# Two attention layers and two gated layers on one core: token statistics moved ahead of phi, transposes one unit ahead, and the copies of k^T v times output weights on ScalarE alone

## The chip, the cores and the metric

The kernel runs on one core of one Trainium2 chip. The time is device microseconds (us) of one execution, as a median of several. TensorE is the matmul engine, VectorE and ScalarE work element by element, GpSimd (POOL in the profile) does small vectors here, and a sequencer (SP) issues the DMA transfers. Each engine is given its own list of instructions, so a schedule is the order in which the program emits them.

## The reference, cut to what matters

```python
phi = lambda t: jnp.where(t > 0, t + 1, jnp.exp(t)) + 1e-6
pq, pk = phi(q), phi(k)
kv  = jnp.einsum("bhsd,bhse->bhde", pk, v)
num = jnp.einsum("bhqd,bhde->bhqe", pq, kv)
den = jnp.einsum("bhqd,bhd->bhq", pq, pk.sum(over tokens))    # shortened
attention(x) = (num / den) @ wo                               # 32 heads of 32
...
x = x + attention(layernorm(x));  x = x + gated(layernorm(x))   # and both once more
```

There are 2048 tokens of width 1024, in bf16. The kernel handles the tokens in 16 tiles of 128, in four groups of four tiles. A tile's layernorm needs its mean and variance ("token statistics") before the tile can be normalised, transposed and multiplied by the weights.

## The kernel before: the parts that the change touches

The k projection of a tile is two units, each eight matmuls, followed by phi on ScalarE (the exp) and VectorE (two instructions):

```python
def phi(ps, dst):
    e = work.tile([P, NB], BF16, tag="e", bufs=3, name="e")
    nc.scalar.activation(out=e[:], in_=ps[:], func=ACT.Exp)
    nc.vector.tensor_scalar(out=e[:], in0=e[:], scalar1=1.0, scalar2=1e-6, op0=ALU.min, op1=ALU.add)
    nc.vector.scalar_tensor_tensor(out=dst, in0=ps[:], scalar=1.0 + 1e-6, in1=e[:], op0=ALU.add, op1=ALU.max)
```

Statistics are made on VectorE (`bn` twice, then an aggregate) and finished on GpSimd (`rstd`). One tile of each later group has its statistics on ScalarE instead (`ln_stats_act`), with GpSimd between its two passes. Group 0 is normalised on VectorE and transposed on TensorE (`tx_pe`, with a ScalarE copy out of PSUM). The later groups are normalised on ScalarE, which first needs an offset from GpSimd, and transposed by a DMA (`tx`).

```python
def ln_apply_act(t, xn):
    mv, rstd = stat.pop(t)
    off = small.tile([P, 1], F32, tag="off", name="off")
    nc.gpsimd.tensor_scalar(out=off[:], in0=mv[:, 0:1], scalar1=rstd[:], scalar2=-1.0, op0=ALU.mult, op1=ALU.mult)
    nc.scalar.activation(out=xn, in_=X[:, t, :], func=ACT.Identity, scale=rstd[:], bias=off[:])
```

The first layer's order, from group 1 on (`u` are projections of the group before):

```python
for g in range(1, NG):
    t = g * TPG
    u = early if g == 1 else k[8 * g - 8:8 * g]
    ... # loads of later tiles of x
    ln_stats(t)
    ln_stats_act(t + 1, xn_a[t + 1])
    u[0]();  norm(t);      ln_stats(t + 2)
    u[1]();  norm(t + 1);  ln_stats(t + 3)
    u[2]();  norm(t + 2)
    ...
    u[3]();  norm(t + 3)
    do(u[4:])
do(k[8 * NG - 8:])
```

The second part that changes sits later in each attention layer. Sixteen single matmuls, k^T v times the output weights, are woven between the last q projections. Each result is copied out of PSUM, one in four by VectorE:

```python
def kvo_unit(c, n):
    ps = mm_tile()
    nc.tensor.matmul(out=ps[:], lhsT=KVT[0][:, c, :], rhs=wo[n][:, c, :], start=True, stop=True)
    if c % 4 == 3:
        nc.vector.tensor_copy(out=KVo[n][:, c, :], in_=ps[:])
    else:
        nc.scalar.copy(out=KVo[n][:, c, :], in_=ps[:])
```

All matmul results share eight PSUM buffers (`mm_tile`). VectorE is far behind at this point: each pair of q projections brings it some 4.3 us of division work besides the two phis of 0.9 us each, and takes TensorE 3.5 us.

## Time and profile before

| before | value |
|---|---|
| time | 1647.24 us, median of 3 (1647.19 to 1649.03) |
| span of the profiled run | 1646.2 us |
| busy: TensorE, VectorE, ScalarE, GpSimd | 1622.5, 646.2, 266.8, 58.0 us |
| mean granted TensorE clock | 0.999 |

TensorE is busy for 99% of the span, so the change can only touch the remaining 24 us, and the stretches in which TensorE's clock is low, which count as busy. The view that finds the waits is the list of waits of TensorE. Its columns are the waiting engine and line, what it waited for, the sum, the number of waits and the longest. This is the kernel before:

```profile
PE ps L233 <- DMA xT_71<-W_77: 3.9, 1, 3.9
PE ps L233 <- ACT xT_70 L215: 2.2, 2, 1.1
PE ps L233 <- DMA xT_73<-D_84: 2.2, 1, 2.2
...
PE ps L233 <- DVE pq L225: 1.1, 2, 0.5
PE ps L319 <- DVE D_80 L321: 1.1, 2, 0.5
PE pt L214 <- DVE W_76 L194: 0.6, 1, 0.6
PE ps L233 <- ACT D_81 L323: 0.6, 2, 0.3
```

L233 is a projection, xT_71 and xT_73 are the transposed tokens of groups 1 and 3, and L319 is one of the sixteen single matmuls. The four lines with xT or pt belong to the first layer. The other three occur once in each attention layer.

A list of waits does not say which wait sets the time. The chain of waits, followed back from the end, does. In the following piece of it for the kernel before, the columns are start, duration and engine with line, in time order:

```profile
29.01 1.21 DVE st L161 x2
30.24 0.22 DVE mv L165
...
30.83 0.66 POOL rstd L169
...
31.59 0.28 POOL off L201
...
33.04 0.59 ACT e L223
```

Up to 62.4 us the chain hardly touches TensorE after 14.5 us. It runs through statistics (st), GpSimd, ScalarE, phi on VectorE, and statistics again. TensorE's waits are where this chain hands work over.

The timeline of TensorE before shows when that happens. The columns are start, duration, engine, line, instruction, output and inputs, count, and in brackets the idle time before it with its releaser:

```profile
30.68 3.55 PE L233 MATMUL ps<-W_74,xT_71 128*128 128x512 bf16 x8 [3.94 <-DMA xT_71<-W_77]
...
62.37 1.90 PE L233 MATMUL ps<-W_74,xT_73 128*128 128x512 bf16 x8 [2.23 <-DMA xT_73<-D_84]
...
76.19 0.81 PE L245 MATMUL ps<-H,W_76 128*128 128x512 bf16 x3
...
184.22 1.03 PE L319 MATMUL ps<-H,kvt 128*128 128x512 bf16 x4
188.39 1.89 PE L233 MATMUL ps<-D_79,xT_73 128*128 128x512 bf16 x7 [0.55 <-DVE pq L225]
...
191.43 1.89 PE L233 MATMUL ps<-D_78,xT_73 128*128 128x512 bf16 x8 [0.30 <-ACT D_81 L323]
...
194.29 0.59 PE L319 MATMUL ps<-H,kvt 128*128 128x512 bf16 x2 [0.54 <-DVE D_80 L321]
...
196.69 5.34 PE L337 MATMUL ps<-D_80,xT_70 128*128 128x512 bf16 x23
```

Eight projection matmuls normally start 1.73 us before the next eight; after the 3.94 us wait it was 3.39 us, at a granted clock of 0.50 (30.7 to 34.0 us). The line at 76.19 us, the first matmul of x^T k, marks the end of the stage. From 184.22 us (the first single matmul) to 196.69 us (the output projection) TensorE needs 12.47 us.

### The profile page before, as it was taken

Reading aid. Unit: us, or ns where it says so; the run is one execution under the profiler, and the core shown is the slowest. Engines: PE = TensorE matmul, PEld = TensorE weight load, DVE = VectorE, ACT = ScalarE, POOL = GpSimd, SP = SyncE. Lnnn points to the kernel's source line nnn. Section 1 sums busy time; section 2 is a strip of 40 time slices with the busy share of each in tenths; the row PEclk is TensorE's granted clock in tenths of the full one; section 3 lists DMA queues with packets and bytes.
Section 4 is the critical chain, followed back from the end, with each engine's and each line's share of the span. In section 5 each row is a group of like instructions: output and inputs, shape, how many; then the busy total and the mean of one; then the engine's idle time right before and its main releaser. Section 6 shows DMA issues by size and latency. Waiting matters only on the chain.

```text
span 1646.2 us, 18145 instructions
## 1 busy us (share of the span) xinstructions
PE 1622.5 (99%) x7547; PEld 744.7 (45%) x7696; DVE 646.2 (39%) x1050; ACT 266.8 (16%) x444; POOL 58.0 (4%) x159
## 2 busy tenths in 40 slices
PE   8999999999999999999999999999999999999999
PEld 3444444444444444444444444444444444444444
DVE  5789964211311321122676889532132113111111
ACT  5522301100110110011023222011011101100110
POOL 2100000000000000000200000000000000000000
PEclk9999999999999999999999999999999999999999
DMA  5602729630641453041450135394226406421400
GB/s 166 167 13 45 192 40 315 189 102 6 177 152 49 112 170 103 0 154 51 108 149 1 32 71 153 98 336 154 67 68 172 157 23 167 152 78 64 154 4 23
DMA packets 245011, 182.59 MB, mean 111 GB/s; under 512 B 100545, under 2 KB 235713, under 8 KB 244929
## 3 DMA queue, kind: packets, MB, share of 16 engines
q1 hardware_dynamic: 244928, 181.43, 38.3%
q8 instruction: 60, 0.98, 0.3%
q14 instruction: 23, 0.18, 0.0%
HBM read 153.09 MB, written 4.19 MB: 96 GB/s over the span
## 4 chain that ended last, share of the span: by engine, by line
PE 94%; DVE 3%; issue 1%; ACT 1%; POOL 0%; DMA 0%; ACTq 0%; DVEq 0%
PE ps L351 47%; PE ps L368 23%; PE ps L233 10%; PE ps L337 7%; PE ps L245 7%; DVE st L161 1%; DVE H L225 1%; ACT e L223 0%; PE zps L153 0%; DVE pq L225 0%; DVE e L224 0%; DVE D_82 L289 0%; DVE den L291 0%; POOL rstd L169 0%; ACT D_81 L323 0%
## 5 line engine op out<-in xcount | busy, mean ns | idle before, releaser
L355 DVE TENSOR_TENSOR H<-gs,ps 128x512 bf16<-128x512 f32 x224 | 154.1, 688 | 575.2 <-PE ps L351 543.7
L354 ACT COPY gs<-ps 128x512 f32<-128x512 f32 x224 | 131.3, 586 | 1039.4 <-PE ps L351 1016.5
L368 PEld LDWEIGHTS <-H 128*128 128x128 bf16 x1848 | 178.6, 98 | 208.7
L370 DVE TENSOR_TENSOR X<-X,ps 128x512 bf16<-128x512 bf16 (+1 forms) x66 | 44.3, 672 | 319.7 <-PE ps L368 287.5
L223 ACT ACTIVATE e<-ps 128x512 bf16<-128x512 f32 x128 | 75.8, 595 | 174.7 <-PE ps L233 163.4
L351 PEld LDWEIGHTS <-W_75 128*128 128x128 bf16 x640 | 62.6, 98 | 75.5
L351 PEld LDWEIGHTS <-W_74 128*128 128x128 bf16 x640 | 62.6, 98 | 75.5
L351 PEld LDWEIGHTS <-xT_72 128*128 128x128 bf16 x576 | 56.4, 98 | 68.0
L351 PEld LDWEIGHTS <-W_76 128*128 128x128 bf16 x576 | 56.4, 98 | 68.0
L351 PEld LDWEIGHTS <-W_77 128*128 128x128 bf16 x576 | 56.4, 98 | 67.9
L351 PEld LDWEIGHTS <-xT_73 128*128 128x128 bf16 x576 | 56.4, 98 | 67.9
L161 DVE BATCH_NORM_STATS2 st<-X 128x6 f32<-128x512 bf16 x122 | 77.4, 675 | 2.3 <-DMA X<-in_A_x_dram 2.3
L351 PE MATMUL ps<-xT_70,xT_72 128*128 128x512 bf16 x314 | 75.3, 379 | 0.3
L351 PE MATMUL ps<-xT_71,W_76 128*128 128x512 bf16 x314 | 75.3, 379 | 0.3
L351 PE MATMUL ps<-xT_71,W_77 128*128 128x512 bf16 x312 | 75.2, 379 | 0.4
L351 PE MATMUL ps<-xT_70,xT_73 128*128 128x512 bf16 x316 | 75.4, 379 | 0.2
L351 PE MATMUL ps<-xT_70,W_74 128*128 128x512 bf16 x316 | 74.7, 379 | 0.3
L351 PE MATMUL ps<-xT_71,W_74 128*128 128x512 bf16 x314 | 74.6, 379 | 0.4
L351 PE MATMUL ps<-xT_71,W_75 128*128 128x512 bf16 x314 | 74.6, 379 | 0.3
L351 PE MATMUL ps<-xT_70,W_75 128*128 128x512 bf16 x312 | 74.2, 379 | 0.3
L368 PE MATMUL ps<-D_81,H 128*128 128x512 bf16 (+2 forms) x264 | 66.0, 373 | 0.4
L368 PE MATMUL ps<-D_78,H 128*128 128x512 bf16 (+2 forms) x262 | 65.9, 372 | 0.3
(127 smaller groups left out, 1817.1 us busy)
## 6 DMA issues: line engine op xcount, KB each, us to landing
W_74<-in_B_w_gate_dram SPq DMA_DIRECT2D x20, 1024.0 KB, 5.3
W_75<-in_B_w_up_dram SPq DMA_DIRECT2D x20, 1024.0 KB, 7.5
W_76<-in_B_w_gate_dram SPq DMA_DIRECT2D x18, 1024.0 KB, 5.3
W_77<-in_B_w_up_dram SPq DMA_DIRECT2D x18, 1024.0 KB, 7.5
xT_72<-in_B_w_gate_dram SPq DMA_DIRECT2D x18, 1024.0 KB, 5.4
xT_73<-in_B_w_up_dram SPq DMA_DIRECT2D x18, 1024.0 KB, 7.1
X<-in_A_x_dram SPq DMA_DIRECT2D x16, 256.0 KB, 4.5
H<-in_A_wo_dram SPq DMA_DIRECT2D x4, 1024.0 KB, 7.1
```

Of the source, the lines that this page charges most:

```text
L161: nc.vector.bn_stats(out=stat[t][0][:, c, :], in_=X[:, t, c * NB:(c + 1) * NB])
L223: nc.scalar.activation(out=e[:], in_=ps[:], func=ACT.Exp)
L225: nc.vector.scalar_tensor_tensor(out=dst, in0=ps[:], scalar=1.0 + 1e-6, in1=e[:], op0=ALU.add, op1=ALU.max)
L233: nc.tensor.matmul(out=ps[:], lhsT=xt[:, k, tl * P:(tl + 1) * P], rhs=w[:, k, :], start=(k == 0), stop=(k == KD - 1))
L245: nc.tensor.matmul(out=ps[:], lhsT=xn_a[t][:, j * P:(j + 1) * P], rhs=pk[t][:, n * NB:(n + 1) * NB], start=(t == 0), stop=(t == NT - 1))
L337: nc.tensor.matmul(out=ps[:], lhsT=xT[t // TPG][:, c, tl * P:(tl + 1) * P], rhs=KVo[n][:, c, :], start=(c == 0), stop=(c == KD - 1))
L351: nc.tensor.matmul(out=ps[:], lhsT=w[:, k, j * P:(j + 1) * P], rhs=xT[g % 2][:, k, :], start=(k == 0), stop=(k == KD - 1))
L354: nc.scalar.copy(out=gs[:], in_=gp[:])
L355: nc.vector.tensor_tensor(out=hT[:, f, :], in0=gs[:], in1=up[:], op=ALU.mult)
L368: nc.tensor.matmul(out=ps[:, 0:hi - lo], lhsT=hT[:, f, tl * P:(tl + 1) * P], rhs=wd[f][:, cols], start=(f == 0), stop=(f == KF - 1))
L370: nc.vector.tensor_tensor(out=X[:, t, cols], in0=X[:, t, cols], in1=ps[:, 0:hi - lo], op=ALU.add)
```

## The change

The intent is to keep TensorE from waiting in the first layer. Statistics of the next tiles go ahead of phi in VectorE's list, TensorE does each transpose of group 0 one projection earlier (tile 3's two), and the copies of the sixteen matmuls leave VectorE, which is behind. The diff, with the loads of x cut:

```diff
-        if c % 4 == 3:
-            nc.vector.tensor_copy(out=KVo[n][:, c, :], in_=ps[:])
-        else:
-            nc.scalar.copy(out=KVo[n][:, c, :], in_=ps[:])
+        nc.scalar.copy(out=KVo[n][:, c, :], in_=ps[:])
...
             ln_apply(1, xn_a[1])
-            k[0]()
             tx_pe(xn_a[1], 1)
             bn(2, 1)
             moments(2)
+            bn(3, 0)
             ln_apply(2, xn_a[2])
+            bn(3, 1)
+            moments(3)
+            ln_stats(4)
+            k[0]()
+            tx_pe(xn_a[2], 2)
+            ln_apply(3, xn_a[3])
             k[2]()
-            tx_pe(xn_a[2], 2)
-            ln_stats(3)
-            ln_apply(3, xn_a[3])
+            tx_pe(xn_a[3], 3)
+            ln_stats_act(5, xn_a[5])
+            norm(4)
+            ln_stats(6)
             k[1]()
+            norm(5)
+            ln_stats(7)
             ... # loads of tiles 8, 9
             k[4]()
-            tx_pe(xn_a[3], 3)
-            early = [k[i] for i in (3, 5, 6, 7)]
-            for g in range(1, NG):
+            norm(6)
+            k[3]()
+            norm(7)
+            ... # loads of tiles 10, 11
+            do(k[5:8])
+            for g in range(2, NG):
```

Groups 2 and 3 keep their order.

More of the change, by code (lines that the diff above doesn't have):

```diff
@@ L409, in layer_A @@
             moments(2)
+            bn(3, 0)
             ln_apply(2, xn_a[2])
+            bn(3, 1)
[4 more added lines that the diff above has]
+            ln_apply(3, xn_a[3])
             k[2]()
-            tx_pe(xn_a[2], 2)
-            ln_stats(3)
-            ln_apply(3, xn_a[3])
+            tx_pe(xn_a[3], 3)
+            ln_stats_act(5, xn_a[5])
+            norm(4)
+            ln_stats(6)
             k[1]()
+            norm(5)
+            ln_stats(7)
+            load_x(8)
+            load_x(9)
             k[4]()
-            tx_pe(xn_a[3], 3)
-            early = [k[i] for i in (3, 5, 6, 7)]
-            for g in range(1, NG):
+            norm(6)
+            k[3]()
+            norm(7)
+            load_x(10)
+            load_x(11)
+            do(k[5:8])
+            for g in range(2, NG):
                 t = g * TPG
-                u = early if g == 1 else k[8 * g - 8:8 * g]
-                load_x(t + 4) if g < 3 else None
-                load_x(t + 5) if g < 3 else None
+                u = k[8 * g - 8:8 * g]
                 ln_stats(t)
+                if g == 2:
+                    load_x(12)
+                    load_x(13)
                 ln_stats_act(t + 1, xn_a[t + 1])
@@ L433, in layer_A @@
                 norm(t + 2)
-                load_x(t + 6) if g < 3 else None
-                load_x(t + 7) if g < 3 else None
                 u[3]()
                 norm(t + 3)
+                if g == 2:
+                    load_x(14)
+                    load_x(15)
                 do(u[4:])
```

## The prediction

> **What bounds it now.** TensorE: busy 1622.5 of 1646.2 us (busy table), 94% of the chain that ended last. Only some 24 us are not matmul, so no schedule change can reach 2% (33 us). The waits of TensorE put the movable part in two places:
> - First-layer k projection (7.4 to 76 us): 2.2 us for copies of transposes, 0.6 for a normalised tile, 3.9 for the first DMA transpose of token group 1 (26.7 to 30.7 us), 2.2 for that of group 3 (to 62.4). After the 3.9 us gap the granted clock was 0.50 from 30.6 to 34.1 us: eight matmuls took 3.5 us, not 1.73. The Trainium skill, "TensorE: Matmul & The Clock Gate" (Part 1), says idle windows of about 3.4 us halve the clock; the trace agrees (3.9 us gap: halved; 2.2 us gap: not).
> - k^T v times output weights, in each attention layer: 0.55 + 0.30 + 0.54 = 1.4 us (timeline, 184 to 197 us and 995 to 1008), waits for PSUM buffers held by VectorE's backlog and its own late copy (193.55 us). Two layers: 2.8 us.
>
> But the chain of waits shows that from 14.5 to 62.4 us it runs VectorE phi -> statistics -> GpSimd -> ScalarE -> DMA transpose. TensorE's waits before 62.4 us count only if that chain shortens.
>
> **Change 1, first layer**, walked with the trace's durations (phi 0.93, pair of statistics 1.21 + 0.2, aggregate to normalise 1.2, exp 0.49 apart, ScalarE normalise 1.14, transpose issue to use 3.15, projection 1.73 us).
> - Tile 3 was issued at 5.2 us and landed 7.8 us later, at 13.0. Its statistics now stand before tile 2's normalise: VectorE waits for it from about 9.8 to 13.0; tile 2's transpose comes at about 14.2 (15.1 before), tile 3's at 17.9 (19.2). TensorE idles about 2.8 us before the former, 1.3 before the latter; projections of group 0 end near 28.7 us (26.7 before).
> - Group 1: ScalarE normalises tile 4 at 23.2 (26.2), transpose issues at 24.5 (27.5), usable at 27.6. The 3.9 us wait and its half clock go: group 1 starts near 28.7 at full speed, 5.5 us of matmul ahead of before.
> - Taken back: ScalarE still has three exps after the four normalises, so statistics of tile 8 start near 35.0 (34.6 before). From there the loops are unchanged and no wait in them is for TensorE: the chain repeats, shifted by +0.35. TensorE now waits about 2 us for group 2 at 42.5; group 3 is usable at 62.7 (62.4), after about 4 us idle. By the window's position about one chance in three that the clock halves there, costing 1.7.
> Net: +0.35, with the clock about +0.9 us.
>
> **Change 2.** ScalarE gains 4 copies per layer (0.49 us apart), VectorE loses 4 (0.60). Counting PSUM buffers, all eight are then never full: 1.4 us per layer go. ScalarE keeps pace (one exp and four copies, 2.5 us, against 2.6 of matmul). -2.6 us for both layers.
>
> **Prediction: 1645.5 us, 80% range 1642.5 to 1648.5.** Faster by over 2%: 1%; within: 98.5%; slower: 0.5%.
>
> **What would show it.** Waits of TensorE: the group 1 wait gone, about 3 us before tile 2's transpose, 2 at group 2, 4 at group 3; VectorE waits about 3 us for X at 10 us; statistics of tile 12 still near 53 us; group 3 starts near 62.7. The waits around k^T v times output weights gone.
>
> **What would make it wrong.** Tile 3 landing sooner or later moves everything up to 62 us one for one; group 2's chain depending on TensorE after all, so that its 5 us lead is kept (up to 6 us faster); the clock halving at the early gap too (+1.2); ScalarE's extra copies delaying the PSUM release of the last q projections.

## The result, and the profile after

The changed kernel took 1646.14 us, median of 4 (1643.60 to 1647.33), against 1647.28 us for the kernel before. The ratio is 0.9989, 95% interval 0.9971 to 1.0006. Ratios here are the mean time of one kernel's runs over that of the other's of the same rounds, so they are not quite the ratio of the quoted medians. Five more runs on another occasion gave 1644.83 us (1644.12 to 1646.76) and 0.9985 (0.9972 to 0.9997). The first interval includes no change at all, the second only just excludes it. By the medians the change is worth 1 to 3 us of 1647, which is the same time by a 2% measure.

The list of waits of TensorE, changed kernel, whole:

```profile
PE pt L214 <- DVE W_76 L194: 5.3, 3, 2.9
PE ps L233 <- DMA xT_73<-D_84: 4.1, 1, 4.1
PE ps L233 <- DMA xT_72<-XW: 2.2, 1, 2.2
PE zps L153 <- DVE xT_73 L150: 1.2, 1, 1.2
```

The 3.9 us wait for group 1 is gone and so are the waits around the sixteen matmuls. In their place stand 2.9 us before tile 2's transposes, 2.2 us before group 2 and 4.1 us before group 3. The timeline of TensorE, changed kernel:

```profile
44.76 1.90 PE L233 MATMUL ps<-W_74,xT_72 128*128 128x512 bf16 x8 [2.20 <-DMA xT_72<-XW]
...
62.81 3.59 PE L233 MATMUL ps<-W_74,xT_73 128*128 128x512 bf16 x8 [4.07 <-DMA xT_73<-D_84]
66.20 2.64 PE L233 MATMUL ps<-W_75,xT_73 128*128 128x512 bf16 x8
...
79.04 1.03 PE L245 MATMUL ps<-H,W_76 128*128 128x512 bf16 x4
...
187.08 1.03 PE L319 MATMUL ps<-H,kvt 128*128 128x512 bf16 x4
...
197.44 5.34 PE L334 MATMUL ps<-D_80,xT_70 128*128 128x512 bf16 x24
```

Group 1 ran ahead of before: its second projection started at 30.31 us, against 34.07. But group 3 starts 0.44 us later than before (62.81 against 62.37). The lead of 3.8 us was not kept. In this execution the first sixteen matmuls of group 3 then ran slowly, so the stage ended at 79.04 us, 2.85 us later than before. The sixteen single matmuls and their projections now take 10.36 us (187.08 to 197.44), not 12.47.

The table by windows of the changed kernel shows why group 3 was slow. The stretch comes first, then its length, then busy time and count for TensorE, its weight loads, VectorE, ScalarE and GpSimd. After the fifth pair come the granted clock, the DMA share and GB/s:

```profile
58.00:62.00 4.00, 0.75 (x4) 0.13 (x2) 3.83 (x9) 2.09 (x3) 1.49 (x5) 0.86 0.29 56
62.00:66.00 4.00, 3.19 (x8) 1.19 (x9) 1.75 (x5) 3.24 (x5) 1.32 (x4) 0.50 0.39 75
66.00:70.00 4.00, 4.00 (x16) 1.61 (x15) 3.27 (x8) 3.50 (x6) 0.00 (x0) 0.79 0.84 148
```

The clock was 0.50 after the idle stretch, as it had been after the group 1 wait before. And VectorE's timeline, changed kernel, shows the wait that the prediction had expected, for the load of tile 3:

```profile
13.00 0.69 DVE L161 BATCH_NORM_STATS2 st<-X 128x6 f32<-128x512 bf16 x1 [3.21 <-DMA X<-in_A_x_dram]
```

### The profile page after: what moved, and what is told of

Read it like the earlier page. It is cut to its first block, busy times and chain, and to the rows that moved or that the text cites. A ratio compares the mean times of both kernels' runs of the same rounds, so it can differ in the third digit from the quotient of the medians.

```text
span 1645.1 us, 18292 instructions
## 1 busy us (share of the span) xinstructions
PE 1629.4 (99%) x7696; PEld 744.8 (45%) x7696; DVE 641.3 (39%) x1042; ACT 270.4 (16%) x452; POOL 57.7 (4%) x159
## 4 chain that ended last, share of the span: by engine, by line
PE 96%; DVE 1%; issue 1%; DMA 1%; ACT 1%; POOL 0%; SPq 0%; ACTq 0%; DVEq 0%
PE ps L348 47%; PE ps L365 24%; PE ps L233 11%; PE ps L334 7%; PE ps L245 7%; DVE H L225 0%; DMA X<-in_A_x_dram 0%; PE ps L310 0%; PE ps L319 0%; DVE st L161 0%; SPq L103 0%; ACT e L223 0%; DMA xT_73<-D_84 0%; DVE e L224 0%; POOL rstd L169 0%
```

## The experiments

Theory A is that of the prediction. The first layer is set by a chain over statistics, GpSimd, ScalarE and phi, so a gain for TensorE counts only where this chain gets shorter; the gain of the change is in the copies. Its rivals are named with each run. All kernels gave correct results. Each was timed five times against the kernel before, whose medians in these rounds were 1647.61 to 1647.73 us.

| run | median us (lowest to highest) | ratio to before (95%) |
|---|---|---|
| a0_change: the change again | 1644.83 (1644.12 to 1646.76) | 0.9985 (0.9972 to 0.9997) |
| e1_copies_only | 1643.18 (1643.11 to 1644.10) | 0.9974 (0.9961 to 0.9987) |
| e2_first_only | 1650.10 (1648.71 to 1652.26) | 1.0015 (1.0003 to 1.0028) |
| e3_tile2_first | 1645.68 (1643.48 to 1647.22) | 0.9988 (0.9974 to 1.0002) |
| e4_tiles34_early | 1641.82 (1641.77 to 1643.48) | 0.9965 (0.9951 to 0.9979) |
| e5_stats_early | 1643.15 (1642.57 to 1643.30) | 0.9970 (0.9957 to 0.9982) |
| e6_warm_fill | 1645.02 (1644.96 to 1647.37) | 0.9986 (0.9974 to 0.9999) |
| e7_copies_8 | 1656.46 (1655.17 to 1657.68) | 1.0050 (1.0037 to 1.0062) |
| e8_all_three | 1641.00 (1639.73 to 1641.44) | 0.9958 (0.9944 to 0.9971) |
| e9_group_ahead | 1642.70 (1642.64 to 1643.08) | 0.9971 (0.9958 to 0.9983) |
| e10_offset_early | 1635.12 (1635.07 to 1635.22) | 0.9923 (0.9910 to 0.9935) |
| e11_e8_offset | 1635.63 (1635.48 to 1635.88) | 0.9926 (0.9912 to 0.9939) |

One reading holds for all of them. Take the start of the first matmul of x^T k, the end of the first stage, from the time of the same profiled execution. What is left is 1567.6 to 1567.9 us in all eleven executions with the copies on ScalarE alone, 1571.8 us in the two with four copies on VectorE (the kernel before and e2_first_only), and 1579.4 us with eight. So every difference between these runs lies either in the first stage or in the copies, and the four copies cost about 4 us over both layers (the kernel before against e1_copies_only: 4.0; e2_first_only against the change: 3.9).

### The change once more

> The changed kernel itself once more, for more runs. In its first profile TensorE idled 4.1 us before token group 3, the clock was halved from about 61 to 68 us, and the k^T v times output weights waits were gone. Theory A (chain of statistics sets the first layer: +0.4; copies: -2.8; a clock that halves or not in that idle time: 0 or +2.4): two clusters of times, near 1644.5 us where the mean granted clock is 0.999 and near 1647 us where it is 0.997 or 0.998. Rival B (the spread is only noise): times do not follow the granted clock.

The two clusters did not appear. The profiled run, in which the clock was halved at group 3, was the slowest at 1646.76 us; the other four lay between 1644.12 and 1645.13 us, three of them with the same mean clock of 0.998. So within these five the mean clock of a run does not tell what a halved stretch cost. Rival B is not shown by that: in e3_tile2_first below, the five times do follow the clock, from 1643.48 us at 1.000 to 1647.22 us at 0.997. The run of e2_first_only below shows that a halved clock at group 2 costs nothing at the end, because TensorE then waits less before group 3.

The profile gave a second reading. Tile 3 landed at 12.6 us here (issued at 5.19, 7.4 us to landing) and at 13.0 in the first profile (5.44 and 7.5). Group 3 started at 62.41 us here and at 62.81 there, so the whole 50 us of chain moved with the load.

### The copies alone, on the kernel before

```diff
-        if c % 4 == 3:
-            nc.vector.tensor_copy(out=KVo[n][:, c, :], in_=ps[:])
-        else:
-            nc.scalar.copy(out=KVo[n][:, c, :], in_=ps[:])
+        nc.scalar.copy(out=KVo[n][:, c, :], in_=ps[:])
```

> Before, with the sixteen copies of each layer all on ScalarE and nothing else changed. Theory A: the three waits of TensorE around those copies (1.4 us in each attention layer) go, -2.8 us against before, about 1644.5 us, the first layer as before (group 1 wait 3.9 us, group 3 wait 2.2 us). Rival B (the copies move nothing, the gain came from the first layer): within 0.5 us of before.

It took 1643.18 us. The ratio of 0.9974 on 1647.7 us is -4.3 us, one and a half times the expected -2.8. The copies alone beat the whole change. The timeline of TensorE in this run gives the size:

```profile
184.32 1.03 PE L319 MATMUL ps<-H,kvt 128*128 128x512 bf16 x4
...
194.68 1.67 PE L334 MATMUL ps<-D,xT 128*128 128x512 bf16 x7
```

From start to start this is 10.36 us, against 12.47 before: 2.11 us for each layer, 4.2 in all. The prediction had summed the listed idle times, 0.55 + 0.30 + 0.54 = 1.39 us. The listed idle time is counted from an end of the last matmul that lies about 0.17 us after the moment at which the next one could have started: eight matmuls are shown as 1.89 to 1.90 us long, but the next eight start 1.73 us after them when nothing waits. Three waits hide 0.5 us in this way. Another 0.25 us is between the two matmuls at 194.29 us before: the pair needs 0.43 us, and the next projection started 0.68 us after it, at 194.97. The Trainium skill, "Perfetto Trace Analysis", section "Tensor Engine Instruction (MATMUL, LD_WEIGHTS)", says that the reported end of a matmul is an estimate from its size and not an observation. This trace agrees in that the listed ends overlap the next starts, and here this correction is 0.5 us on a listed sum of 1.39 us.

### The first-layer order alone

The changed kernel with the four old lines of the copies put back (the diff above, reversed).

> The first-layer reordering alone, copies shared with VectorE as before. Theory A: group 3 starts 0.4 us later than before, so +0.4 us against before without the halved clock and about +2.9 us with it: 1647.5 to 1650 us, not faster than before; the copy waits of 1.4 us per layer stay. Rival B (the reordering is what gains): 2 to 4 us below before.

It took 1650.10 us, and the ratio of 1.0015 is +2.5 us: the reordering by itself makes the kernel slower. Rival B is out. The timeline of TensorE in this run:

```profile
63.10 13.99 PE L233 MATMUL ps<-W,xT 128*128 128x512 bf16 x62 [1.78 <-DMA xT<-D]
76.93 1.89 PE L245 MATMUL ps<-H,W 128*128 128x512 bf16 x8
```

In its profile group 3 started at 63.10 us, with tile 3 landed at 13.2 (5.20 + 8.0), and the stage ended at 76.93 us, +0.74 against before. In that run the clock was halved at group 2 (0.50 from 47 to 49 us), where it did no harm, because TensorE's wait for group 3 shrank to 1.78 us. The slower runs of this kernel (up to 1652.26 us, with a mean clock of 0.997) have no profile, so it is only argued that a halved clock in group 3 made them slow. If the 1571.8 us after the first stage hold for them too, their first stage ended at up to 80.5 us (an estimate).

### Tile 2's normalise ahead of tile 3's statistics

```diff
             moments(2)
-            bn(3, 0)
             ln_apply(2, xn_a[2])
+            bn(3, 0)
             bn(3, 1)
```

> The changed kernel with both statistics halves of tile 3 put behind tile 2's normalise, so that tile 2 no longer waits for tile 3's load. Theory A (only the chain over VectorE's statistics counts): TensorE's 2.9 us wait for tile 2 almost goes, but tile 3's normalise comes only about 0.4 us earlier, and group 3 starts about 0.4 us earlier (62.4 instead of 62.8 us): -0.4 us against the changed kernel. Rival B (TensorE's waits count one for one): group 3 or the end of the stage 2 to 3 us earlier.

The median was 1645.68 us against 1644.83 for the change in the same rounds, with overlapping ranges: no gain. In the profile TensorE's 2.9 us wait for tile 2 vanished and one of the same length (2.79 us) stood before tile 3's transposes. Group 3 started at 61.98 us. Tile 3 landed at 12.4 us in this run, so about 0.6 us of the 0.83 us that this lies under the first profile of the change is the load. What the order itself gives is small, as A expected. But the run is a weak test of rival B: the wait was moved from tile 2 to tile 3 rather than removed, and the listed waits before TensorE's transposes fell by only 1.3 us in sum (4.0 against 5.3). The clock was also halved in group 0 here (0.50 at 17 to 20 us), as in the profiles of e5_stats_early and e6_warm_fill.

### Tiles 3 and 4 loaded sooner

```diff
+    load_x(3)
+    load_x(4)
     for k in range(0, KD, 4):
         load(wk[1][:, k:k + 4, :], wqkv_v[:, k:k + 4, D + NB:2 * D])
-    for t in range(3, 2 * TPG):
+    for t in range(5, 2 * TPG):
         load_x(t)
```

> The changed kernel with the loads of tiles 3 and 4 issued ahead of the second half of the k weights, so that they land about 2.4 us sooner. Theory A (tile 3's landing sets the chain one for one): tile 2's transposes near 11.5 us instead of 14.2, group 2 usable near 42.3 (44.8), group 3 near 60.3 us (62.8), about -2.5 us against the changed kernel with the same clock pattern, about 1642.5 us. Rival B (tile 3's landing only hurts TensorE locally and the later waits absorb it): group 3 still near 62.5 us, time unchanged.

The timeline of TensorE in this run:

```profile
41.88 15.67 PE L235 MATMUL ps<-W,xT 128*128 128x512 bf16 x63 [2.13 <-DMA xT<-XW]
60.00 6.20 PE L235 MATMUL ps<-W,xT 128*128 128x512 bf16 x20 [2.45 <-DMA xT<-D]
```

Group 2 started at 41.88 us (44.76 in the change) and group 3 at 60.00 (62.81): 2.8 to 2.9 us earlier, nearly one for one with a tile 2 transposed about 2.8 us sooner (at 11.4 instead of 14.2 us). The time was 1641.82 us, 3.0 us under the change. Rival B is out: with the load late, the change had put a wait for it at the head of the chain. Tile 4 and the second half of the k weights moved with tile 3, and their shares were not separated.

The run also shows the clock falling from full to half. Its windows after the 2.13 us wait:

```profile
42.00:44.00 2.00, 2.00 (x7) 0.75 (x6) 0.99 (x2) 1.24 (x2) 1.21 (x4) 0.65 0.45 87
44.00:46.00 2.00, 2.00 (x6) 0.72 (x5) 0.99 (x2) 2.00 (x4) 0.00 (x0) 0.50 0.41 79
```

A wait of 2.13 us came before a halved clock here, which set in at about 42.6 us, 0.7 us after TensorE had started again. In the kernel before, a wait of 2.23 us did not.

### First statistics of groups 2 and 3 ahead of the last phis

```diff
             norm(7)
             load_x(10)
             load_x(11)
+            ln_stats(8)
+            ln_stats_act(9, xn_a[9])
             do(k[5:8])
             for g in range(2, NG):
-                ln_stats(t)
-                ln_stats_act(t + 1, xn_a[t + 1])
                 ...
                 if g == 2:      # the block that loads tiles 14, 15
+                    ln_stats(t + 4)
+                    ln_stats_act(t + 5, xn_a[t + 5])
                 do(u[4:])
```

> The changed kernel with the statistics of the first two tiles of groups 2 and 3 put ahead of the last phis of the group before, on VectorE and ScalarE; loads as in the changed kernel. Theory A (TensorE's lead of 5.5 us is lost because those statistics wait behind phis): no or almost no wait for group 2 (TensorE there at 42.4 us, transpose landed near 41.9), group 3 starts near 57 us instead of 62.8, idle before it at most 1.5 us, so the clock is not halved; about -5.5 us without and -8 us with a halved clock in the run compared, near 1638 us. Rival B (the transposes or something else set the pace): group 3 near 62 us still, time within 1 us of the changed kernel.

The time was 1643.15 us, only 1.7 us under the median of the change, where 5.5 to 8 had been expected. Neither theory was right. TensorE's waits in this run, without those of group 0:

```profile
PE ps L233 <- DVE H L225: 2.8, 1, 2.8
...
PE ps L233 <- DMA xT<-XW: 1.1, 1, 1.1
PE ps L233 <- DMA xT<-D: 0.3, 1, 0.3
```

Group 2's first tile was in time, but its second was not (1.1 us), and then TensorE had no free PSUM buffer for 2.8 us, since phi was behind. ScalarE, which makes phi's exps, stood idle for 3.3 us before it could normalise tile 9, waiting for that tile's offset on GpSimd.

### Matmuls of no use in the idle time before group 3

```diff
+            fill = mm_tile()
+            for i in range(14):
+                nc.tensor.matmul(out=fill[:], lhsT=xT[0][:, 0, 0:P], rhs=xT[0][:, 0, :], start=True, stop=True)
             do(k[8 * NG - 8:])
```

> The changed kernel with 14 matmuls of no use (3 us) put ahead of the projections of group 3, in TensorE's idle time there. Theory A (the idle time before group 3 halves the clock and costs up to 2.4 us in some runs): group 3 starts at the same time, near 62.6 us, but its eight projections run at 1.73 us each; mean time 0.5 to 2 us below the changed kernel, with less spread. Rival B (the clock does not depend on that idle time): first projections of group 3 slow as before, times unchanged or higher.

In three of the five runs the mean clock was 1.000, which no run of the change had shown, and these lay within 0.03 us of one another (1644.96 to 1645.02). That suggests that the spread of the change comes with its idle time; the other two runs still differ by 1.2 and 2.4 us. But the mean, 1645.7 us, is not below that of the change (1645.1 in its own rounds, before-means 1647.9 and 1647.7). The profiled run, at 1647.37 us the slowest, shows a cost of the means:

```profile
47.12 15.67 PE L233 MATMUL ps<-W,xT 128*128 128x512 bf16 x63 [2.41 <-DMA xT<-XW]
62.63 3.19 PE L455 MATMUL ps<-xT 128*128 128x512 bf16 x13
65.66 13.98 PE L233 MATMUL ps<-W,xT 128*128 128x512 bf16 x63
```

This run was late from the head of the chain: tile 3 landed at 13.65 us (13.00 in the change), the clock was halved in group 0 (0.50 from 14.0 to 20.8 us), and ScalarE normalised tile 12 at 60.22 us, 1.76 us later than in the change. The clock was halved again at group 2, and TensorE came to the filling late. Without the filling, group 3 could have started near 64.6 us (an estimate: 62.81 plus 1.76); it started at 65.66 us, so the filling cost about 1.1 us. Group 3 itself then ran at full speed. As a measure of what the halved clock costs on average the run is inconclusive.

### Twice as many copies on VectorE

```diff
+        if c % 2 == 1:
+            nc.vector.tensor_copy(out=KVo[n][:, c, :], in_=ps[:])
+        else:
+            nc.scalar.copy(out=KVo[n][:, c, :], in_=ps[:])
-        nc.scalar.copy(out=KVo[n][:, c, :], in_=ps[:])
```

> The changed kernel with eight of the sixteen copies of each layer on VectorE (before: four, change: none). Theory A (copies behind VectorE's backlog hold PSUM buffers and stop TensorE): the out projection of the first layer starts 4 to 5 us later than in the changed kernel relative to the first of these matmuls; 4 to 10 us above the changed kernel in all, 1650 to 1655 us. Rival B (which engine copies does not matter so long as TensorE has buffers): within 1 us of the changed kernel.

It took 1656.46 us, 11.6 us above the change of the other rounds and a little beyond the expected range. The timeline of TensorE in this run:

```profile
186.31 1.03 PE L319 MATMUL ps<-H,kvt 128*128 128x512 bf16 x4
...
196.38 3.53 PE L233 MATMUL ps<-D,xT 128*128 128x512 bf16 x8 [1.22 <-DVE D L321]
...
202.79 12.47 PE L337 MATMUL ps<-D,xT 128*128 128x512 bf16 x56
```

The stretch is 16.48 us with eight copies on VectorE, 12.47 with four and 10.36 with none. A copy itself takes much the same on either engine (0.68 us on VectorE, 0.60 on ScalarE in the profile before). What costs is that the buffer is freed only when VectorE's backlog has been worked off. At 196.38 us TensorE stands still for exactly such a copy, and the waits also leave its clock halved for those eight matmuls (3.53 us).

### Loads and statistics together

The diffs of e4_tiles34_early and e5_stats_early on top of the change.

> The changed kernel with both the earlier loads of tiles 3 and 4 and the statistics ahead of the last phis. The run with the statistics alone gained 1.5 us only: TensorE waited for tile 9 (GpSimd works in order, and tile 9's offset stood behind tile 10's statistics) and then 2.8 us for a PSUM buffer behind VectorE's phis. Theory A' (the chain sets the stage wherever it is shortest of time, and the landing of tile 3 shifts all of it): the 2.5 to 3 us of the earlier loads add to the 1.5 of the statistics, about 4 us below the changed kernel, near 1640.5 us. Rival B' (VectorE's amount of work is what is left, so the earlier loads add nothing to the earlier statistics): no better than the better of the two, near 1642 us.

It took 1641.00 us: 3.8 under the median of the change, but only 0.8 under the earlier loads alone. TensorE still waited 2.7 us for a PSUM buffer and 1.1 us for another. The time lies nearer to A' (1640.5 us) than to B' (1642 us), and all five times lie below all five of e4_tiles34_early. But the waits for buffers stayed, so this run did not settle the two theories.

### All statistics one group ahead

All loads of x stand at the start, tiles 3 and 4 as in e4_tiles34_early. The loop becomes:

```diff
+            norm(4); ln_stats(6); ln_stats(7)
+            k[1]();  norm(5);  ln_stats(8)
+            k[4]();  norm(6)
+            k[3]();  norm(7);  ln_stats_act(9, xn_a[9])
+            k[5]();  ln_stats(10)
+            k[6]();  k[7]();   ln_stats(11)
             for g in range(2, NG):
+                ahead = g + 1 < NG
                 u[0]();  norm(t)
                 u[1]();  norm(t + 1);  # + ln_stats(t + 4) if ahead
                 u[2]();  norm(t + 2);  # + ln_stats_act(t + 5, ...) if ahead
                 u[3]();  norm(t + 3);  # + ln_stats(t + 6) if ahead
                 do(u[4:6]);            # + ln_stats(t + 7) if ahead
                 do(u[6:])
```

> The changed kernel with all loads of x issued at the start (tiles 3 and 4 ahead of the second half of the k weights) and the statistics of each group of four tiles spread over the projections of the group before the one that needs them, so that no normalise waits for a statistic just computed. Theory A' (what is left is the order, the latency of statistics between phis, not VectorE's amount of work): no wait of TensorE above 0.5 us after group 0, the xk matmuls start near 67.5 to 69 us (76.2 before, 76.4 to 79 in the changed kernel), time near 1635 us. Rival B' (VectorE's amount of work): PSUM waits of TensorE of some us come in their place, xk near 74 us, time near 1641 us.

It took 1642.70 us, and TensorE waited 3.7 us for a transpose of group 2. The expectation of A' missed by almost 8 us, and the PSUM waits of some us of B' did not come either (one of 0.6 us), though its 1641 us was nearer. The list of waits of ScalarE between 30 and 66 us names the cause:

```profile
ACT XW L205 <- POOL off L203: 8.8, 3, 5.3
ACT D L205 <- POOL off L203: 2.3, 1, 2.3
```

ScalarE waited 5.3 us for one offset of a [128, 1] vector. GpSimd's timeline in the same run shows where that offset stood:

```profile
34.60 0.23 POOL L169 TENSOR_SCALAR ve<-mv 128x1 f32<-128x1 f32 x1 [2.14 <-DVE mv L167]
...
37.84 0.22 POOL L169 TENSOR_SCALAR ve<-mv 128x1 f32<-128x1 f32 x1 [2.21 <-DVE mv L167]
...
38.80 0.50 POOL L203 TENSOR_SCALAR off<-mv,rstd 128x1 f32<-128x1 f32 x2
```

The offset of tile 8 was emitted with tile 8's normalise, so it stood behind the statistics of tiles 10 and 11, which waited for VectorE, although its own inputs had been ready since 25.7 us. Moving statistics ahead had moved GpSimd's waits ahead of its useful work. The Trainium skill, "PSUM — Partial Sum Buffer", section "Engine vs sequencer instructions", says: "ScalarE/VectorE/GpSimdE queues are strict FIFO." The trace agrees: GpSimd idled 2.14 and 2.21 us with a ready instruction behind a waiting one.

### The offset directly behind its statistics

```diff
+    def offset(t):            # the four lines of ln_apply_act that make off, on GpSimd, with bufs=2 * TPG
+        ...
+        stat[t] = (mv, rstd, off)
...
             ln_stats(8)
+            offset(8)         # and so for tiles 4 to 15, after each ln_stats and ln_stats_act
```

> The run with the statistics a group ahead missed its forecast: ScalarE waited 5.3 us for tile 8's offset on GpSimd, which works in order and had the statistics of tiles 10 and 11 ahead of it, and 2.7 us for tile 10's. Here every offset is computed directly behind its tile's statistics, and nothing else differs from that run. If that order on GpSimd was the cause: ScalarE's waits for offsets of tiles 8 to 15 fall under 1 us each, tile 8 is normalised near 34 us (39.1), TensorE waits for nothing above 0.6 us after group 0, xk starts near 70 us (75.1), time near 1637.5 us. If VectorE's amount of work is the cause: PSUM waits of some us in their place, xk near 74, time near 1642 us.

It took 1635.12 us, 12.5 under the kernel before, better than expected, with a spread of 0.15 us over five runs and a clock of 1.000 in each. The list of TensorE's waits, whole:

```profile
PE pt L222 <- DVE W L196: 3.3, 3, 1.8
PE zps L155 <- DVE xT L152: 1.2, 1, 1.2
```

and its timeline from 15.42 us to the end of the stage:

```profile
15.42 51.96 PE L241 MATMUL ps<-W,xT 128*128 128x512 bf16 x240
67.22 1.89 PE L253 MATMUL ps<-H,W 128*128 128x512 bf16 x8
```

All thirty projections after group 0's first two run without a break. Tile 8 was normalised at 30.0 us instead of 39.1, and ScalarE no longer waits for any offset. VectorE does the same work as before, so its amount of work was not the limit of this stage. The larger number of buffers for the offsets, which the edit needs, is no rival: in e9_group_ahead GpSimd waited for no such buffer.

### The same on the smaller reordering

The `offset` edit on e8_all_three.

> The best kernel so far (earlier loads of tiles 3 and 4, first statistics of groups 2 and 3 ahead of the last phis) with every offset directly behind its tile's statistics. In it TensorE still waited 1.1 and 2.7 us for PSUM buffers, behind phis whose exps stood behind the normalises of tiles 9 and 13, which waited for the offsets. If GpSimd's order is the cause of these: they shrink to under 1.5 us in sum, xk near 71 us (73.6), time near 1638.5 us. If VectorE's amount of work is the cause: unchanged, near 1641 us.

It took 1635.63 us, and the 1.1 and 2.7 us PSUM waits shrank to one of 0.2. So the place of twelve small GpSimd instructions was worth 5.4 us to e8_all_three and 7.6 us to e9_group_ahead. Statistics a whole group ahead add only 0.5 us to that. Whether the offsets alone would have done as much for the changed kernel was not run and stays open.

## Why the prediction was right

The total was right: 1645.5 us predicted, 1646.14 and 1644.83 measured, inside the range of 1642.5 to 1648.5. The mechanism was right, too, but the closeness of the total is partly luck: two sizes were wrong in opposite directions.

1. **What bounds the first layer: right.** The prediction said that TensorE's waits before 62.4 us count only if the chain over statistics and phi shortens. Group 1 started at full speed at 28.59 us, where 28.7 had been stated. (The "5.5 us of matmul ahead" was a slip: the start is 2.1 us earlier and the slow clock 1.65 us less, which makes 3.8.) Group 3 started at 62.81 us, where 62.7 had been stated. Taking TensorE's largest remaining wait away from tile 2 (e3_tile2_first) only moved it to tile 3 and gained nothing, and shortening the head of the chain by 2.8 us (e4_tiles34_early) gained 3.0.
2. **The wait for tile 3: right.** VectorE waited 3.21 us until 13.00 us (about 9.8 to 13.0 had been stated), and the start of group 3 followed that tile one for one: in the four profiles with the order and the loads of the change, its first statistics started at 12.57, 12.93, 13.00 and 13.26 us and group 3 at 62.41, 62.77, 62.81 and 63.10.
3. **The clock: right in kind, too small.** The prediction gave it one chance in three and 1.7 us (an estimate whose working it did not give), and read a threshold from two waits of the kernel before (3.9 us: halved; 2.2 us: not), which e4_tiles34_early did not bear out (2.13 us, then halved). In the first profile it cost 2.4 us (the stage ended 2.85 us late, of which 0.44 was the chain). The reordering alone was +2.5 us by e2_first_only, and +1.7 us at the median from e1_copies_only to a0_change, where "+0.35, with the clock about +0.9 us" had been predicted. How much of the excess is clock was not settled.
4. **The copies: right in kind, too small.** The step was "1.4 us per layer go", from the listed idle times. From start to start it was 2.11 us for each layer, and for both -4.3 us by the timed runs (about 4 by the profiles) where -2.6 had been predicted. The mis-sized term is the listed idle of a matmul wait, which leaves out about 0.17 us each, and one stall inside a merged pair of matmuls.
5. **What the prediction did not see.** It took the chain as a property of VectorE's order. Its slack was in GpSimd's. e10_offset_early showed that offsets emitted beside their use, behind other tiles' statistics, cost 7.6 us in a kernel whose statistics were all in time.

## What to carry to other kernels

Before moving work ahead on one engine, walk the lists of all engines that the moved work passes through: an instruction moved forward carries its wait with it, and everything behind it on an in-order engine waits along, even on an engine that is 4% busy. A lead of the busiest engine is worth nothing if a later stage makes it wait for a chain that did not move, so ask what ends the last wait of the stage and not the longest one. Size a removed matmul wait from start to start of the matmuls around it, and time the parts of a change one by one, since here one part was worth -4.3 us and the other +2.5.

## What the Trainium skill lacked or had wrong

- "TensorE: Matmul & The Clock Gate", Part 1, lets the clock halve after an idle window of about 3.4 us. In these runs listed waits of 2.13 us (e4_tiles34_early) and 2.41 us (e6_warm_fill) were followed by a clock of 0.50, while waits of 2.20 us (the change) and 2.23 us (before) were not. In the change, even 2.85 us in group 0 was not, and the clock before group 3 fell at about 60.9 us, when TensorE had been idle for 2.15 us. The page's free-running window may explain that the result varies, which no run here shows; an idle time well below 3.4 us can be enough.
- "Perfetto Trace Analysis", section "Tensor Engine Instruction (MATMUL, LD_WEIGHTS)", says that a matmul's end is estimated, but not that idle times taken from it come out too short. Here eight matmuls were listed 0.17 us longer than their spacing, and three waits listed as 1.39 us cost about 1.9; another 0.25 us of the 2.11 us was a stall inside a merged line, which is not listed at all.
- "PSUM — Partial Sum Buffer", section "Engine vs sequencer instructions", states that GpSimd's queue is strictly first in, first out. No page read draws the consequence for small helper instructions: their place in the list was worth 5.4 and 7.6 us here.
